# Moving five preparation pieces and thinning the feed-forward queue around steps 258 to 290 of a fused attention and feed-forward kernel

## The chip, the cores and the metric

The kernel runs on one core of a Trainium2 chip. The metric is the device time of one execution in microseconds; shown times are the median of several runs of the same kernel. TensorE does the matrix products, ScalarE the exponentials and tanh, VectorE the work on small tiles and most of what reads TensorE's results, GpSimd some element-wise work, and SyncE issues most of the transfers.

## The reference

Two parts follow each other. The first is attention in which a query only sees the keys of its own cluster; the second is a gated feed-forward layer on its output.

```python
# batch 4, heads 8, sequence 768, head size 64, 16 clusters
q_assign = argmax(normalised q . normalised centroids)      # and the same for k
scores = where(q_assign == k_assign, (q @ k.T) / sqrt(64), -1e9)
out = softmax(scores) @ v
x = out as 3072 x 512
y = (sigmoid(x @ w_gate) * (x @ w_val)) @ w_out             # 512 -> 1536 -> 512
```

## The kernel before

The work is cut into 384 **steps**, which TensorE takes in order. Batch 0 has steps 0 to 95, batch 1 has 96 to 191, batch 2 has 192 to 287 and batch 3, the last, 288 to 383. In batches 1 to 3 a pair of heads takes 24 steps: pair 0 of batch 3 begins at step 288, pair 1 at 312. A step multiplies one 128-key chunk of a head with 384 queries (tile `sc`, line 893), lets ScalarE take the exponential (`es`, line 898), and multiplies the `es` of an earlier step with V (three matmuls into `av`, line 916, two steps behind in these batches). So TensorE's order is `sc`, some feed-forward work, `av`, some preparation, and then the next step. After the last `av` of a head or head pair, VectorE and GpSimd normalise (`t` line 370, `rec` line 372, `xp` line 375), and a transposing transfer brings the result to `xTb` (line 947), the feed-forward layer's input.

**The feed-forward queue.** The feed-forward work stands in a queue of pieces, each with a cost in nanoseconds that was written by hand: `g` (four matmuls of 384 columns, line 530, then a tanh `th`, line 536), `v` (four matmuls, line 546, then a VectorE product into `hT`, line 551), and pieces of the output product (`o`, line 821, three matmuls of 256 columns each). At each step the function `ffn_run(ns)` adds `ns` to a credit and takes pieces from the queue while the credit is positive. The number is `ns` plus the batch plus the quarter of the batch: `ns23` holds for batch 2, fourth quarter, steps 264 to 287. What a step does not take stays in the queue for later steps, and what is left at the end runs after the last step; all pieces run in any case. A `g` piece of batch 2's first half is entered in the queue at step 283.5, behind the pieces that still wait there.

The output product of a half batch runs as seven products k = 0 to 6 into two long-lived accumulators, x and y; each product has four `o` pieces. Products 0, 2, 4 and 6 go to x, the others to y. Behind a product a VectorE or ScalarE operation reads the accumulator: ScalarE after k = 0, VectorE (line 768) after all others, twice after k = 4. Product 5 adds to y and so must wait until the operation behind k = 3 has read y.

**The banks.** `sc`, `g`, `v`, most small results (`lg`, line 434; `vs_ps`, line 341) share one pool of four accumulator banks (`ring`). A new tile in it waits until the reader of the tile that had the bank is done: the exponential for `sc`, the tanh for `g`, line 551 for `v`, line 449 for `lg`, line 346 for `vs_ps`.

**The preparation.** What a head pair needs before its first step is cut into named pieces, and each piece has a step offset in the table `SCHED`, relative to the first step of the pair. A name such as `b3p1lg0` is batch 3, pair 1, piece `lg` of head 0; where a batch has no entry of its own, that of batch 2 holds for batches 2 and 3. The pieces of this change are

- `lg`: twelve small matmuls (line 434) of the transposed keys and queries with the centroids. They need `T`, which a transposing transfer (line 410) brings.
- `pk`: the assignment from them, all on VectorE (lines 449, 460, 462 twice, 469), into a tile that a later piece transposes.
- `vs`, `vu`, `vt`: the sum over all V rows; `vs` is one VectorE addition (line 330), `vu` two more (lines 336 and 337), `vt` one matmul (line 341) and one VectorE operation (line 346).

Every engine takes its instructions in the order in which this program wrote them, so a piece that stands early on VectorE and waits keeps what is behind it waiting.

Of the kernel before, what the change touches and what calls it, by code (L numbers as in the profile page):

```python
# [59 lines left out]
    "b1p2vs": -11.0, "b1p2vu": -2.5, "b1p2vt": 3, "b1p2ld": -67.5, "b1p2l20": 1.5, "b1p2le0":  # L60
    2.0, "b1p2l21": 0, "b1p2le1": 2.0, "b1p3sp00": -60.5, "b1p3sp01": -54.0, "b1p3tn0": -51,
    "b1p3lg0": -38.0, "b1p3pk0": -36.5, "b1p3sp10": -55.0, "b1p3sp11": -43.0, "b1p3tn1":
    -40.0, "b1p3lg1": -29, "b1p3pk1": -27.0, "b1p3ot": -23.5, "b1p3hp0": -13.0, "b1p3hp1":
    -12.5, "b1p3vc": -7.5, "b1p3vs": -18.5, "b1p3vu": -14.5, "b1p3vt": 4, "b1p3ld": -69.5,
    "b1p3l20": 0, "b1p3le0": -4.0, "b1p3l21": 0, "b1p3le1": 1.0, "b2sp00": -57.5, "b2sp01":
    -54, "b2tn0": -49.5, "b2lg0": -39, "b2pk0": -39, "b2sp10": -50.0, "b2sp11": -44.5,
# [11 lines left out]
    "xs13": 0, "sd": 1, "b2lk": -0.5, "b1lk0": 2.0, "b1lk1": -9, "b1lk2": -0.5, "b1lk3": -1.5,  # L78
    "b2lq": 0, "b1lq0": 2.5, "b1lq1": -0.5, "b1lq2": 1.0, "b1lq3": -4.5, "b2lv": 1.0, "b1lv0":
    -1, "b1lv1": 0.5, "b1lv2": 0.5, "b1lv3": 1.5, "ns02": 490, "ns03": 490, "ns20": 500,  # L80
    "ns21": 491, "ns22": 481, "ns23": 491, "ns30": 443, "ns31": 443, "ns32": 443, "ns33": 423,
    "h6hi1E": "P", "h1ev1E": "A", "g1hi0E": "A", "h3hi1E": "P", "g1lo0E": "D", "h1lo0E": "D",
    "r3pl0E": "A", "hM3": 0, "hM7": 1, "h1hi0E": "P", "g1hi1E": "P", "h3ev0E": "A", "g0pl0E":
    "A", "g1pl0E": "A", "hM2": 1, "g1ev0E": "A", "wq": 6, "b2p1lk": 8, "b2p1lq": 8, "b2p1lv":
# [7 lines left out]
    "g0pl1E": "A", "kc": 3, "r2ev1E": "A", "g1pl1E": "A", "vso32": 1, "r0ev1E": "A", "vso31":  # L92
    1, "tx": 1, "b2p3lk": 8.5, "b2p3lq": 9, "b2p3lv": 10, "b3p3lk": 8.5, "b3p3lq": 9,
    "b3p3lv": 10,
}


# [1493 lines left out]
```

## Time and profile before

| what | us |
|---|---|
| median of 3 runs (322.22 to 323.26) | 322.86 |
| the profiled execution | 323.67 |
| its span, first to last instruction | 321.9 |
| TensorE busy | 314.6 |
| ScalarE busy | 231.1 |
| VectorE busy | 224.9 |
| GpSimd busy | 108.6 |

In the profile's rows PE is TensorE's matmul, PEld its weight load, DVE is VectorE, ACT is ScalarE, POOL is GpSimd and SP is SyncE; a q behind the name is the engine's sequencer. A row of the timeline has the start, the length, the engine, the line, the operation, the tiles it writes and reads with their shapes, and how many instructions it joins; brackets tell the idle time before it. Because matmuls overlap, a TensorE row's length reaches into the next row; what a group costs is read from one start to the next.

### The profile page before, as it was taken

Reading aid. Unit: us, or ns where it says so; the run is one execution under the profiler, and the core shown is the slowest. Engines: PE = TensorE matmul, PEld = TensorE weight load, DVE = VectorE, ACT = ScalarE, POOL = GpSimd, SP = SyncE. Lnnn points to the kernel's source line nnn. Section 1 sums busy time; section 2 is a strip of 40 time slices with the busy share of each in tenths; the row PEclk is TensorE's granted clock in tenths of the full one; section 3 lists DMA queues with packets and bytes.
Section 4 is the critical chain, followed back from the end, with each engine's and each line's share of the span. In section 5 each row is a group of like instructions: output and inputs, shape, how many; then the busy total and the mean of one; then the engine's idle time right before and its main releaser. Section 6 shows DMA issues by size and latency. Waiting matters only on the chain.

```text
span 321.9 us, 9181 instructions
## 1 busy us (share of the span) xinstructions
PE 314.6 (98%) x3510; PEld 222.4 (69%) x3510; DVE 224.9 (70%) x598; ACT 231.1 (72%) x521; POOL 108.6 (34%) x145
## 2 busy tenths in 40 slices
PE   7999999999999999999999999999999999999996
PEld 5888666766666666666777687566777688667775
DVE  5799656777787677576878587586767356456666
ACT  6688988787888888877867866778877886332320
POOL 6877464154434365433133333414211111000000
PEclk9999999999999999999999999999999999999999
DMA  7999997738876996978884751942503112200103
GB/s 214 374 256 180 244 171 118 210 75 236 238 113 187 163 238 155 223 172 136 108 219 115 217 113 33 314 110 52 111 2 90 40 26 79 77 2 1 65 2 131
DMA packets 77709, 45.16 MB, mean 140 GB/s; under 512 B 56865, under 2 KB 75105, under 8 KB 77665
## 3 DMA queue, kind: packets, MB, share of 16 engines
q1 hardware_dynamic: 73696, 39.73, 49.7%
q0 software_dynamic: 3680, 4.72, 9.0%
q8 instruction: 27, 0.44, 0.6%
q10 hardware_dynamic: 288, 0.13, 0.2%
q14 instruction: 18, 0.14, 0.2%
HBM read 28.34 MB, written 6.29 MB: 108 GB/s over the span
## 4 chain that ended last, share of the span: by engine, by line
PE 89%; DMA 3%; DVE 3%; issue 2%; POOL 1%; SPq 0%; ACT 0%; POOLq 0%; DVEq 0%
PE g L530 19%; PE v L546 19%; PE sc L893 17%; PE av L916 10%; PE o L821 8%; PE o L684 5%; PE lg L434 2%; PE o_end L594 2%; DMA T<-hl 2%; PE lg L421 1%; PE t_ps L1142 1%; PE o L594 1%; DMA xTb<-xp 1%; PE oh_ps L1202 1%; DMA qraw<-in_q_dram 1%
## 5 line engine op out<-in xcount | busy, mean ns | idle before, releaser
L898 ACT ACTIVATE es<-sc 128x384 f16<-128x384 f32 x384 | 174.3, 492 | 40.6 <-PE sc L893 31.9
L893 PE MATMUL sc<-T 128*128 128x384 f16 x384 | 117.8, 326 | 0.4 <-DVE T L1223 0.4
L916 PEld LDWEIGHTS <-es 128*128 128x128 f16 x1152 | 81.3, 98 | 35.9 <-issue 0.8
L916 PE MATMUL av<-va,es 128*128 128x65 f16 x1152 | 97.6, 194 | 0.0
L551 DVE SCALAR_TENSOR_TENSOR hT<-th,v 128x384 f16<-128x384 f32 x96 | 53.0, 553 | 55.6 <-PE av L916 36.0
L530 PE MATMUL g<-xTb,wg 128*128 128x384 f16 x384 | 78.2, 326 | 0.7 <-DMA xTb<-xp 0.5
L546 PE MATMUL v<-xTb,wv 128*128 128x384 f16 x384 | 78.1, 326 | 0.0
L536 ACT ACTIVATE th<-g 128x384 f32<-128x384 f32 x96 | 47.2, 491 | 35.0 <-PE g L530 15.9
L375 POOL TENSOR_TENSOR xp<-t,rec 128x384 f16<-128x384 f32 (+1 forms) x30 | 21.6, 720 | 101.8 <-DVE rec L372 52.3
L530 PEld LDWEIGHTS <-wg 128*128 128x128 f16 x384 | 37.2, 97 | 19.3 <-issue 0.4
L546 PEld LDWEIGHTS <-wv 128*128 128x128 f16 x384 | 37.4, 98 | 18.6
L893 PEld LDWEIGHTS <-T 128*128 128x128 f16 x384 | 37.1, 97 | 0.6 <-DVE T L1223 0.5
L1459 POOL TENSOR_TENSOR hl<-kraw,hl 128x384 f16<-128x384 f32 x22 | 20.2, 920 | 41.1 <-DVE hl L1458 20.5
L1459 POOL TENSOR_TENSOR hl<-qraw,hl 128x384 f16<-128x384 f32 x22 | 20.9, 950 | 9.8 <-DVE hl L1458 9.8
L768 DVE TENSOR_TENSOR ob<-o,ob 128x256 f32<-128x256 f32 (+1 forms) x35 | 17.8, 523 | 7.6 <-PE o L821 6.8
L370 DVE TENSOR_TENSOR t<-av,sv 128x390 f32<-128x390 f32 (+1 forms) x30 | 14.4, 479 | 9.7 <-PE av L916 7.3
L821 PEld LDWEIGHTS <-sum 128*128 128x128 f16 x168 | 16.4, 98 | 5.2 <-issue 0.8
L684 PE MATMUL o<-wo,hT 128*128 128x512 f16 x72 | 19.9, 379 | 0.0
L821 PE MATMUL o<-wo,hT 128*128 128x256 f16 x126 | 19.8, 272 | 0.0
L449 DVE TENSOR_REDUCE lgs<-lg 128x192 f32<-128x384 f32 x23 | 12.7, 551 | 2.8 <-PE lg L434 2.7
L821 PEld LDWEIGHTS <-hT 128*128 128x128 f16 x126 | 12.2, 97 | 3.4
L322 POOL CAST va<-vraw 128x768 f16<-128x768 f32 x15 | 13.0, 869 | 1.9 <-DMA vraw<-in_v_dram 1.9
(158 smaller groups left out, 340.1 us busy)
## 6 DMA issues: line engine op xcount, KB each, us to landing
vraw<-in_v_dram SPq DMA_DIRECT2D x15, 384.0 KB, 4.9
kraw<-in_k_dram SPq DMA_DIRECT2D x14, 384.0 KB, 4.3
qraw<-in_q_dram SPq DMA_DIRECT2D x12, 384.0 KB, 4.2
out_dram<-ob SPq DMA_DIRECT2D x18, 256.0 KB, 2.4
wg<-in_moe_w_gate_dram POOLq DMA_DIRECT2D x2, 768.0 KB, 9.5
wv<-in_moe_w_val_dram POOLq DMA_DIRECT2D x2, 768.0 KB, 10.3
wo<-in_moe_w_out_dram POOLq DMA_DIRECT2D x2, 768.0 KB, 9.3
T<-ohT SPq DMA_DIRECT2D x44, 24.0 KB, 1.9
```

The lines of the kernel that those rows point to most:

```text
L375: (eng or POOL).tensor_tensor(x, t[:, 0:nq, 0:64], bcast(rec[:, 0:nq], 64), ALU.mult)
L530: PE.matmul(out=g[:, 0:n], lhsT=wg[fc // WQ][:, dc, fc % WQ, :], rhs=xT[:, dc, t0 : t0 + n], start=(dc == 0), stop=(dc == NDC - 1),)
L536: ACT.activation(th[:, 0:n], g[:, 0:n], AF.Tanh)
L546: PE.matmul(out=w[:, 0:n], lhsT=wv[fc // WQ][:, dc, fc % WQ, :], rhs=xT[:, dc, t0 : t0 + n], start=(dc == 0), stop=(dc == NDC - 1),)
L551: DVE.scalar_tensor_tensor(HB[b, blk][:, fc, 0:n], st[0][:, 0:n], 1.0, w[:, 0:n], ALU.add, ALU.mult)
L684: PE.matmul(out=o, lhsT=HB[b, blk][:, fc, bass.ts(t, 128)], rhs=wo[fc // WON][:, fc % WON, :], start=(fc == 0), stop=(fc == NFC - 1),)
L768: plus = lambda dst, a, z: DVE.tensor_tensor(dst, a, z, ALU.add)
L821: PE.matmul(out=st[z][:, e], lhsT=a[:, c, :], rhs=rhs[:, c, :], start=start and c + e == 0, stop=c == HF - 1, skip_group_check=True,)
L893: PE.matmul(out=sc.rearrange("p (c t) -> p c t", t=128), lhsT=s["k"], rhs=s["q"], start=True, stop=True,)
L898: ACT.activation(es, sc, AF.Exp, scale=SCALE)
L916: PE.matmul(out=av[:, a0 + s["c0"] + i, :], lhsT=s["es"][:, bass.ts(i, 128)], rhs=VA[b, p][:, e, s["j"], :], start=(first and i == 0 and a ...
L1459: POOL.tensor_tensor(hl[:, :, 64:128], r, hl[:, :, 0:64], ALU.subtract)
```

## The change

Six entries of the table are new or changed. Nothing is computed differently; no instruction is added or left out.

```diff
-    "b1p3lg0": -38.0, "b1p3pk0": -36.5, ... "b1p3lg1": -29, "b1p3pk1": -27.0,
+    "b1p3lg0": -38.0, "b1p3pk0": -36.5, ... "b1p3lg1": -28, "b1p3pk1": -27.0,
...
-    "ns21": 491, "ns22": 481, "ns23": 491,
+    "ns21": 491, "ns22": 481, "ns23": 410,
...
+    "b3p0vs": -30, "b3p0vu": -28, "b3p0vt": -9, "b3p1lg0": -32, "b3p1pk0": -32, "END": 0,
```

In steps:

| piece | before | after |
|---|---|---|
| batch 1, pair 3: `lg1` | 139 | 140 |
| batch 3, pair 0: `vs` | 269 | 258 |
| batch 3, pair 0: `vu` | 271 | 260 |
| batch 3, pair 0: `vt` | 290 | 279 |
| batch 3, pair 1: `lg0`, `pk0` | 273 | 280 |
| credit per step, steps 264 to 287 | 491 ns | 410 ns |

The entry `END` is read by nothing. The smaller credit withholds 24 x 81 ns = 1,944 ns of hand-written cost, so that from step 265 on the queue's pieces stand later than before, by one to three steps at first; the first `g` of batch 2's first half moves from step 284 to 286, and of the last output product of batch 2 seven `o` pieces instead of three stand in step 383 or behind it.

4 rows, old and new, of the table SCHED are left out of this document.

## The prediction

> **What bounds the kernel now.** I read the page's first part, then TensorE's busy time by stretch, then the matmul rows in order, looking for places where the next start comes later than the matmul before it allows.
>
> ```profile
> PE 314.6 (98%) x3510; PEld 222.4 (69%) x3510; DVE 224.9 (70%) x598; ACT 231.1 (72%) x521; POOL 108.6 (34%) x145
> ```
> ```profile
> 184.60:204.70 20.10, 18.94 (x226) 15.06 (x225) 15.86 (x42) 13.13 (x28) 7.69 (x10) 1.00 0.48 122
> 224.00:313.00 89.00, 89.00 (x812) 62.86 (x811) 53.62 (x121) 51.30 (x112) 8.60 (x12) 1.00 0.16 45
> ```
>
> TensorE is the bound; no other engine is over 72%. In the second stretch (from step 315 on) it shows no idle time; in the first (steps 264 to 287, the ones whose queue is thinned) it misses 1.2 of 20.1 us. The order of TensorE's work changes, its amount does not, so the change can win or lose only holes, and I price it hole by hole. I first need what a step costs, from one start to the next:
>
> ```profile
> 182.74 0.81 PE L530 MATMUL g<-xTb,wg 128*128 128x384 f16 x4
> 183.38 0.26 PE L916 MATMUL av<-va,es 128*128 128x65 f16 x3
> ...
> 183.89 0.81 PE L546 MATMUL v<-xTb,wv 128*128 128x384 f16 x4
> 184.54 0.25 PE L916 MATMUL av<-va,es 128*128 128x65 f16 x3
> 184.63 0.33 PE L893 MATMUL sc<-T 128*128 128x384 f16 x1
> ```
> ```profile
> 194.68 0.49 PE L821 MATMUL o<-vheld,sum 128*128 128x256 f16 x3
> 195.78 0.49 PE L821 MATMUL o<-wo,sum 128*128 128x256 f16 x3 [0.62 <-DVE ob L768]
> 196.11 0.26 PE L916 MATMUL av<-va,es 128*128 128x65 f16 x3
> 196.20 0.32 PE L893 MATMUL sc<-T 128*128 128x384 f16 x1
> ```
> ```profile
> 200.02 0.45 PE L434 MATMUL lg<-cm,T 128*128 128x32 f16 x12
> 200.32 0.32 PE L893 MATMUL sc<-T 128*128 128x384 f16 x1
> 200.48 0.65 PE L530 MATMUL g<-xTb,wg 128*128 128x384 f16 x3
> 201.68 0.32 PE L530 MATMUL g<-xTb,wg 128*128 128x384 f16 x1 [0.54 <-DMA xTb<-xp]
> ```
>
> So g or v costs 0.65 (0.16 a matmul), an o piece 0.33 (195.78 to 196.11), av 0.09, sc 0.16 (200.32 to 200.48), lg 0.30. Two holes are already visible: in step 277 the next o could start at 194.68 + 0.33 = 195.01 and starts at 195.78, **0.77 lost**; in step 284 the fourth matmul of g could start at 200.48 + 3 x 0.16 = 200.97 and starts at 201.68, **0.71 lost**. The two others:
>
> ```profile
> 99.02 0.26 PE L916 MATMUL av<-va,es 128*128 128x65 f16 x3
> 99.41 0.36 PE L434 MATMUL lg<-cm,T 128*128 128x32 f16 x8
> ```
> ```profile
> 205.96 0.81 PE L546 MATMUL v<-xTb,wv 128*128 128x384 f16 x4
> ...
> 207.01 0.32 PE L893 MATMUL sc<-T 128*128 128x384 f16 x1
> 207.49 0.81 PE L530 MATMUL g<-xTb,wg 128*128 128x384 f16 x4
> ```
> ```profile
> 206.88 0.56 DVE hT L551
> 207.44 0.04 issue
> ```
>
> Step 139: lg could start at 99.11 and starts at 99.41, **0.30 lost**, waiting for T's transfer. Step 292: g could start at 207.17 and starts at 207.49, **0.32 lost**: its bank is that of the v two steps earlier, whose reader, line 551, ends at 207.44 (the chain of waits; 0.05 from a reader's end to the matmul). A hole under 0.16 is covered by the modelled ends of the matmuls; by the starts, the stretch from 224 us has one of 0.12 in step 322, the same kind:
>
> ```profile
> 229.46 0.49 PE L821 MATMUL o<-wo,hT 128*128 128x256 f16 x3
> 229.91 0.32 PE L530 MATMUL g<-xTb,wg 128*128 128x384 f16 x1
> ```
>
> **The change part by part.**
>
> *lg1 of batch 1, pair 3, one step later.* Step 140 holds only sc and av, so TensorE reaches lg 0.25 later, when T lacks 0.05. Gain **0.25**. pk1, which reads it, stays a step behind; it gave TensorE no hole.
>
> *lg0/pk0 and vs/vu away from the product: step 277.* The o that lost 0.77 is product 5, which waits until line 768 has read y behind product 3. VectorE's order was:
>
> ```profile
> 192.78 0.26 DVE L336 TENSOR_TENSOR va<-va 128x128 f32<-128x128 f32 x1
> 193.08 0.52 DVE L337 TENSOR_TENSOR vs<-va,va 128x128 f16<-128x128 f32 x1
> 193.52 0.55 DVE L449 TENSOR_REDUCE lgs<-lg 128x192 f32<-128x384 f32 x1
> 194.10 0.35 DVE L460 TENSOR_REDUCE mx<-lgs 128x12 f32<-128x192 f32 x1
> 194.49 0.43 DVE L462 TENSOR_TENSOR oh<-lgs,mx 128x96 f16<-128x96 f32 x2
> 194.95 0.19 DVE L469 TENSOR_SCALAR oh<-oh 128x96 f16<-128x96 f16 x1
> 195.05 1.88 DVE L768 TENSOR_TENSOR ob<-o,ob 128x512 f32<-128x512 f32 x3
> 196.85 0.35 DVE L370 TENSOR_TENSOR t<-av,sv 128x195 f32<-128x195 f32 x1
> 197.23 0.18 DVE L372 RECIPROCAL rec<-t 128x3 f32<-128x3 f32 x1
> ```
>
> From 192.78 to 195.05 VectorE does vu and pk0, 2.27 us, ahead of the 768 that TensorE waits for (its turn was over after one of the three, 0.63 each). Both leave. In the changed order product 3 ends in step 276 and product 5 begins in step 280; between them TensorE has av, all of 277 (one o, 0.58), 278 with two o (0.91), 279 with one o and vt (0.6) and sc of 280, some 2.3 us, for one 768. Gain **0.77**. If that cover went, for instance because the two sums in front of that 768 grew, up to 0.77 would come back. Late next: sc of 283 waits for vt's line 346 behind two 768 (1.26) and sc of 284 for line 449 (0.55); TensorE has about 2.4 and 3.3 us until then, so nothing.
>
> *The thinner queue: step 284.* The o pieces in front of the g are spread over two steps more, and the g itself moves to 286. Its chain begins at t in step 278: t at 196.85, landing 0.04 before 201.68, so 4.79 us, of which the transfer is the largest:
>
> ```profile
> 198.06 3.58 DMA xTb<-xp
> ```
>
> Before, t started 0.65 after sc of 278 (VectorE was at the three 768) and TensorE needed 4.8 from there to the fourth g matmul. After, with one 768 gone ahead, t can start some 0.25 after it, so landing is at about 5.0; TensorE's steps 278 to 285 sum to 0.91 + 0.64 + 0.88 + 0.58 + 0.91 + 0.88 + 0.58 + 0.58 and 286 adds 0.16 + 0.33 + 0.49 until the fourth, 6.9 in all. Gain **0.71**, with 1.9 us to spare. On SP two stores and the load of keys are issued behind this transfer, as before; the 512 KB store moves behind that load, whose keys are first read in step 304.
>
> *vt from 290 to 279: step 292.* It took a bank between v and g. Without it g of 289 and 292 wait for exponentials, as the built program has them. Gain **0.32**. At 279 there are no g and v to rob of a bank.
>
> *What vs and vu cost at their new place.* vs stands in front of a conversion that feeds a transfer needed 20 steps later; vu stands in front of line 449 of another head, whose bank sc of 264 then takes.
>
> ```profile
> L330 DVE TENSOR_TENSOR va<-vraw x12: 523/550/1175, 69.4 to 243.4; 128x384 f32<-128x384 f32 x12
> ```
> ```profile
> L337 DVE TENSOR_TENSOR vs<-va,va x12: 295/296/889, 76.0 to 247.2; 128x128 f16<-128x128 f32 x12
> ```
> ```profile
> 183.22 0.55 DVE L449 TENSOR_REDUCE lgs<-lg 128x192 f32<-128x384 f32 x1
> ```
> ```profile
> 183.59 0.49 ACT L536 ACTIVATE th<-g 128x384 f32<-128x384 f32 x1 [0.16 <-PE g L530]
> ```
>
> Line 449 moves from 183.22 to about 183.8 (0.26 + 0.30), ends at 184.35, and sc of 264 is due at 184.63: hidden; at the longest 337 (0.89) it would end 0.3 late. But the banks are dealt anew: v of step 263, due at 183.89, took the bank that line 449 had freed and now takes that of the g of 261, whose tanh ends at 184.08. It waits until 184.13. Loss **0.24** (bounds 0 and the 0.32 of step 292).
>
> *The shifted rhythm, steps 286 to 383.* All g and v stand a step or more later. In the built program one g repeats the case of step 292: g of 310 takes the bank of v of 308. From v's start to g's start that took 207.49 - 205.96 = 1.53; TensorE's own way is 0.65 + 0.09 + 0.16 + 0.09 + 0.16 = 1.15. Loss **0.38** (bounds 0, if VectorE is early, and twice that). The small hole of 322 I leave in both kernels. The seven o at the end cost what they cost elsewhere, since TensorE is the bound in both places; product 6 there comes about 1.9 us behind the two 768 that it needs (1.26).
>
> **Sum.** -0.25 - 0.77 - 0.71 - 0.32 + 0.24 + 0.38 = **-1.43 us**. The profiled execution would go from 323.67 to 322.2. The median shown is 322.86, 0.81 below it; I take the holes to be in every run and forecast 322.86 - 1.43 = **321.4 us**.
>
> **The rivals.**
>
> *The waits stay where they were.* Product 5 or the transfer is late for another reason, and the steps only wait elsewhere. For it: the 3.58 is well over what other such transfers take.
>
> ```profile
> DMA to landing us min/median/max: 2.3/2.5/4.1
> ```
>
> Against it: even 4.1 fits in the 1.9 us to spare. If one of the two large holes stays, the gain is about 0.7 and the time 322.2; if both, 322.86. Chance 0.17.
>
> *Slower: the bank wait at every turn.* The g that takes the bank of the v two steps back pays up to 0.38 each time. From step 286 to 362 a g stands two steps behind a v at thirteen places, before the change at ten. Four places beyond the one counted eat the gain; from seven on (-1.43 + 7 x 0.38 = +1.2) the kernel is slower, 324.1. For it: the wait exists at 292 and 322, and a VectorE operation in front of line 551 is enough for it. Against it: most of the ten places of before show no hole, since an o or lg in between (0.30 to 0.33) covers the wait, or the g takes the bank of an exponential. Chance 0.13. The Trainium skill's Perfetto Trace Analysis, section Identifying Performance Opportunities, says that a gap repeating on the engine that should be saturated can mean too little PSUM for the next tile; the ring keeps its four banks here, so by that rule the waits would go on and the time would be that 324.1. This case's trace agrees only in part: with the same four banks, 89.00 of 89.00 us from 224 us on show as busy.
>
> *More than forecast.* Neither new wait comes: -2.05, 320.8, or the small holes go too, 320.6. Chance 0.08.
>
> **How the numbers follow.** My forecast has 0.62. Its own range is 320.8 to 321.9: the sum with both new waits at nothing and with 0.5 more. Adding the case where large holes stay gives 322.7 above; runs of one kernel scatter by half a microsecond, which takes the low end to 320.4. A measurement tells this kernel from itself at about 0.3%, 0.97 us; the forecast is -0.44%. Faster by more than that: 0.62 + 0.08 = 0.70; within: 0.17; slower: 0.13.
>
> **What would show it.** Right: no TensorE hole over 0.1 us in steps 277 to 300; lg of 140 starting at most 0.2 behind the start of its av; the fourth g matmul of step 286 right behind the third; line 768 right behind product 3; holes of 0.2 to 0.4 at v of 263 and g of 310. Wrong: a hole at o of 280 or g of 286, or a row of holes at g between 286 and 362 with line 551 as the releaser, or transfers that land over 5.5 us after their issue.

## The result and the profile after

| | before | changed |
|---|---|---|
| median of 22 runs each, us | 322.88 (322.22 to 324.59) | 322.0 (321.42 to 323.41) |
| profiled execution, us | 323.67 | 323.41 |
| its span | 321.9 | 321.6 |
| TensorE busy | 314.6 | 314.1 |

The ratio is 0.997 with a 95% interval of 0.9957 to 0.9982, so the changed kernel is faster by about 1 us (0.003 x 322.88 = 0.97). The forecast was 321.4 us, 1.43 us faster. A later set of 12 runs of the same kernel gave 0.9962 (0.9948 to 0.9976), 1.2 us faster.

In the changed kernel all lines behind the table stand one further down than before (`g` 531, `v` 547, `hT` 552, `sc` 894, `av` 917, `lg` 435, `o` 822, `ob` 769). The page's first part of the changed kernel, then the busy time by stretch: all engines over steps 264 to 287 (the first two numbers are the stretch's length and TensorE's busy time), and TensorE alone from 224 us on:

```profile
PE 314.1 (98%) x3510; PEld 222.1 (69%) x3510; DVE 225.2 (70%) x598; ACT 230.8 (72%) x521; POOL 108.9 (34%) x145
```
```profile
185.98:202.61 16.63, 16.63 (x214) 13.85 (x213) 13.95 (x39) 11.90 (x25) 6.92 (x9) 1.00 0.49 125
```
```profile
224.00:313.00 89.00, 89.00 (x809) 1.00 0.18 45
```

Steps 264 to 287 show no idle time any more; before they missed 1.2 us. In the timeline of the changed kernel, TensorE's rows from the last piece of product 3 to the first of product 5 and around the first `g`, and VectorE's read of y behind product 3:

```profile
194.16 0.49 PE L822 MATMUL o<-kheld,sum 128*128 128x256 f16 x3
194.49 0.25 PE L917 MATMUL av<-va,es 128*128 128x65 f16 x3
194.58 0.33 PE L894 MATMUL sc<-T 128*128 128x384 f16 x1
194.74 0.49 PE L822 MATMUL o<-vheld,sum 128*128 128x256 f16 x3
...
196.71 0.33 PE L894 MATMUL sc<-T 128*128 128x384 f16 x1
196.87 0.49 PE L822 MATMUL o<-wo,sum 128*128 128x256 f16 x3
...
201.29 0.49 PE L822 MATMUL o<-wo,hT 128*128 128x256 f16 x3
201.62 0.81 PE L531 MATMUL g<-xTb,wg 128*128 128x384 f16 x4
202.26 0.26 PE L917 MATMUL av<-va,es 128*128 128x65 f16 x3
```
```profile
194.69 0.69 DVE L769 TENSOR_TENSOR ob<-o,ob 128x512 f32<-128x512 f32 x1 [0.28 <-PE o L822]
```

VectorE's read now starts right behind the product that ends at 194.7, instead of behind preparation work, product 5 starts at 196.87 without a wait (0.16 behind its `sc`), and the four matmuls of the first `g` stand in one row: its fourth no longer waits. Step 140 (start of `lg` 0.09 behind the start of its `av`) has no hole either:

```profile
99.24 0.26 PE L917 MATMUL av<-va,es 128*128 128x65 f16 x3
99.33 0.45 PE L435 MATMUL lg<-cm,T 128*128 128x32 f16 x12
```

The two new waits are where they were forecast, at `v` of step 263 and at `g` of step 310. TensorE's rows, and in a fence of its own ScalarE's tanh whose bank `v` takes, over at 185.19 (184.70 + 0.49):

```profile
184.85 0.33 PE L894 MATMUL sc<-T 128*128 128x384 f16 x1
185.25 0.81 PE L547 MATMUL v<-xTb,wv 128*128 128x384 f16 x4
...
218.55 0.33 PE L894 MATMUL sc<-T 128*128 128x384 f16 x1
219.08 0.81 PE L531 MATMUL g<-xTb,wg 128*128 128x384 f16 x4 [0.20 <-DVE hT L552]
```
```profile
184.70 0.49 ACT L537 ACTIVATE th<-g 128x384 f32<-128x384 f32 x1 [0.16 <-PE g L531]
```

By starts, less the 0.16 of `sc`, that is 0.24 and 0.37. And there is one hole that was not foreseen, in step 177, where the change moves nothing. `lg` could start at 120.52 + 0.09 = 120.61 and starts at 122.06, **1.45 lost**, for a transfer that the chain of waits (the last row) shows with 7.08 us:

```profile
120.52 0.26 PE L917 MATMUL av<-va,es 128*128 128x65 f16 x3
122.06 0.47 PE L435 MATMUL lg<-cm,T 128*128 128x32 f16 x12 [1.29 <-DMA T<-hl]
```
```profile
114.93 7.08 DMA T<-hl
```

From step 132 on the first profile had holes of 0.30 + 0.78 + 0.71 + 0.31 + 0.07 + 0.12 = 2.29 us (the fifth and sixth in steps 298 and 322), the changed one has 0.23 + 0.37 + 1.45 = 2.05. The difference, 0.24, is about what the two executions differ by (0.26). Whether step 177 belongs to the change, and which part of the change removed which hole, is what the experiments had to tell.

### The profile page after: what moved, and what is told of

Read it like the earlier page. It is cut to its first block, busy times and chain, and to the rows that moved or that the text cites. A ratio compares the mean times of both kernels' runs of the same rounds, so it can differ in the third digit from the quotient of the medians.

```text
span 321.6 us, 9181 instructions
## 1 busy us (share of the span) xinstructions
PE 314.1 (98%) x3510; PEld 222.1 (69%) x3510; DVE 225.2 (70%) x598; ACT 230.8 (72%) x521; POOL 108.9 (34%) x145
## 4 chain that ended last, share of the span: by engine, by line
PE 92%; DVE 3%; DMA 2%; ACT 1%; issue 0%; ACTq 0%; POOL 0%; DVEq 0%
PE g L531 20%; PE v L547 19%; PE sc L894 18%; PE av L917 10%; PE o L822 10%; PE o L685 3%; DMA T<-hl 2%; PE lg L435 2%; PE o_end L595 2%; PE lg L422 1%; PE o L595 1%; PE oh_ps L1203 1%; PE t_ps L1143 1%; PE wm L985 1%; PE t_ps L1026 0%
```

## The experiments

The change has seven entries that act, not six: the places of `lg1`, `vs`, `vu`, `vt`, `lg0` and `pk0`, and the credit. Holes below are worked out as in the prediction, from one start to the next, in the profile of each run, from step 132 on. Ratios are against the kernel before, run on the same chip.

**lg1 alone.**

```diff
-"b1p3lg1": -29
+"b1p3lg1": -28
```

> Only lg1 of batch 1, pair 3 is moved from step 139 to 140. Theory (holes on TensorE add up): the hole of 0.30 us at lg of 139 goes, nothing else changes, -0.3 us against the kernel before. Rival (the hole of 1.45 us at lg of step 177 in the changed kernel's profile comes from this move, because everything behind step 139 now asks its transfers 0.3 us earlier): a hole over 1 us at lg of 177 here too, and in most runs, so +0.8 to +1.2 us.

Measured: 0.9995 (0.9978 to 1.0013), no difference. In its profile (TensorE's timeline) the transfer of `T` landed later, and the hole of 139 came back in step 140: `av` starts at 99.10 and ends its 0.09 at 99.19, `lg` starts at 99.66, 0.47 lost. There is no hole in step 177. In step 284 the order is that of before and the hole is 0.41 instead of 0.71.

```profile
99.10 0.26 PE L916 MATMUL av<-va,es 128*128 128x65 f16 x3
99.66 0.47 PE L434 MATMUL lg<-cm,T 128*128 128x32 f16 x12 [0.30 <-DMA T<-hl]
```

A later place does not remove this wait for good; the landing itself moves between executions by more than the step that was won.

**All but lg1.**

```diff
 (the changed kernel)
-"b1p3lg1": -28
+"b1p3lg1": -29
```

> The changed kernel with lg1 put back to step 139. Theory: holes at 139 (0.30), 263 (0.23) and 310 (0.37), none at 177, 277, 284 and 292; -1.1 us against the kernel before, 0.3 slower than the changed kernel. Rival (the lg1 move brings the hole at 177): no hole at 177 and a kernel that is as fast as the changed one or faster than it, -1.0 to -2.0 us.

Measured: 0.9963 (0.9947 to 0.9979). Its holes are 0.39 in step 139, 0.23 in 263 and 0.37 in 310; 177, 277, 284 and 292 have none. The whole gain is there without lg1's move.

**The thinner queue alone.**

```diff
-"ns23": 491
+"ns23": 410
```

> Only the credit of steps 264 to 287 goes from 491 to 410 ns; no piece moves. Theory of the prediction (the hole of 0.77 us at step 277 goes because lg0/pk0 and vs/vu leave VectorE's queue ahead of line 768): that hole stays here, at least in part, and the kernel gains 0.71 at step 284 and little more. Rival (the thinner queue alone gives line 768 the time it needs): no hole at 277 to 280, none at 284, a bank wait of about 0.2 at v of 291 in place of the one of 292, and the 0.37 at 310; -1.2 us, nearly the whole gain of the change.

Measured: 0.9966 (0.9951 to 0.998). The rival was right: with every preparation piece at its old place, the steps from 277 to 286 have no hole. In VectorE's timeline of this kernel (first fence) `pk0` (lines 449 to 469) still stands ahead of the 768 behind product 3, as before; the second fence is TensorE's timeline there, from the last piece of product 3 on, and the third that piece in the kernel before:

```profile
193.25 0.55 DVE L449 TENSOR_REDUCE lgs<-lg 128x192 f32<-128x384 f32 x1
...
194.68 0.19 DVE L469 TENSOR_SCALAR oh<-oh 128x96 f16<-128x96 f16 x1
194.78 0.68 DVE L768 TENSOR_TENSOR ob<-o,ob 128x512 f32<-128x512 f32 x1
```
```profile
193.32 0.49 PE L821 MATMUL o<-kheld,sum 128*128 128x256 f16 x3
...
194.48 0.82 PE L821 MATMUL o<-vheld,sum 128*128 128x256 f16 x6
195.13 0.26 PE L916 MATMUL av<-va,es 128*128 128x65 f16 x3
195.23 0.32 PE L893 MATMUL sc<-T 128*128 128x384 f16 x1
195.39 0.49 PE L821 MATMUL o<-vheld,sum 128*128 128x256 f16 x3
...
195.81 0.33 PE L893 MATMUL sc<-T 128*128 128x384 f16 x1
195.97 0.49 PE L821 MATMUL o<-wo,sum 128*128 128x256 f16 x3
```
```profile
192.61 0.49 PE L821 MATMUL o<-kheld,sum 128*128 128x256 f16 x3
```

But product 5, at 195.97, comes 0.5 us after VectorE's read is over (194.78 + 0.68 = 195.46). The thinner queue moves product 3 later, past preparation that keeps its steps: `vu` is now done ahead of the product, and less of `pk0` is still to come. From the start of product 3's last piece, VectorE's read starts after 1.46 us (194.78 - 193.32) where it was 2.44 before (195.05 - 192.61). TensorE's own way from that piece to product 5 grows only from 2.40 (195.01 - 192.61) to 2.65. What is left is 0.18 in step 291, where `v` takes the bank of a tanh (sc starts at 203.53, `v` at 203.87), 0.37 in step 310 and 0.46 in step 139.

**The pieces alone, without the thinner queue and lg1.**

```diff
+"b3p0vs": -30, "b3p0vu": -28, "b3p0vt": -9, "b3p1lg0": -32, "b3p1pk0": -32,
```

> Only vs, vu, vt, lg0 and pk0 of batch 3 move; lg1 and the credit stay as before. Theory: the holes of 277 (0.77) and 292 (0.31) go, that of 284 stays at about 0.7, that of 263 (0.23) comes, none at 310; -0.85 us. Rival (the transfer at 284 is late only in some executions): a hole at 284 that differs from 0.7 by more than 0.3 in this profile.

Measured: 0.9993 (0.9978 to 1.0008), 0.2 us, where 0.85 had been expected. The hole of 277 is gone, as is that of 292, and 263 shows its 0.23. But part of the gain is lost again in 284, in TensorE's timeline and, for the transfer, the chain of waits:

```profile
199.61 0.65 PE L531 MATMUL g<-xTb,wg 128*128 128x384 f16 x3
201.18 0.32 PE L531 MATMUL g<-xTb,wg 128*128 128x384 f16 x1 [0.92 <-DMA xTb<-xp]
```
```profile
197.17 3.96 DMA xTb<-xp
```

`g` starts 0.87 us earlier than before (200.48 there), its fourth matmul only 0.50 earlier (201.68 there), because it waits for a transfer: 201.18 - 199.61 - 0.49 = 1.08 lost instead of 0.71. The transfer was issued 0.89 earlier as well (197.17 against 198.06), but took 3.96 us and not 3.58: what is gained ahead of a wait for a transfer counts only as far as the transfer lands earlier too. In three profiles with the old places of these pieces and the old credit the hole is 0.71, 0.41 and 0.11, on average 0.41. Against that, this profile gives -0.78 - 0.31 + 0.23 + 0.67 = -0.19 us, near what the runs say; as it is one profile, that the transfer is as late in most runs is argued and not shown.

**The changed kernel again.** No edit.

> The changed kernel once more, for a second profile. Theory (the hole of 1.45 us at lg of step 177 is one execution's late transfer): no hole over 0.5 us at 177, holes of 0.23 at 263 and 0.37 at 310 again, a profiled execution about 1.4 us shorter than the first; -0.9 us or more against the kernel before. Rival (the change brings it): the hole at 177 again, at 1 us or more.

Measured: 0.9962 (0.9948 to 0.9976). The profile has holes in 263 (0.23) and 310 (0.37) alone; 177 has none. TensorE's time from `sc` of step 138 to its last matmul is 219.19 us, against 220.64 in the first profile: the difference is the 1.45 of step 177.

**vt, lg1 and a queue of 420; vs, vu, lg0 and pk0 stay.** The order of the built program deals `v` of 263 and `g` of 310 other banks here, and the credit of 420 was chosen for that.

```diff
-"b1p3lg1": -29   "ns23": 491
+"b1p3lg1": -28   "ns23": 420
+"b3p0vt": -9,
```

> Of the change, lg1 at 140 and vt at 279 are kept; vs, vu, lg0 and pk0 stay where the kernel before has them, and the credit of steps 264 to 287 is 420 instead of 410 ns. Theory (the queue and vt carry the gain; vs and vu bring the bank wait at 263, and the wait at 310 comes from where exactly g and v fall): no hole at 263, 277, 284, 292 and 310, so 0.23 + 0.37 = 0.6 us faster than the changed kernel, -1.5 us or more against the kernel before. Rival (vs, vu and lg0 were needed to free VectorE for line 768): a hole of 0.3 to 0.8 at step 277 to 280 comes back and the kernel is no faster than the changed one.

Measured: 0.9957 (0.994 to 0.9974), that is 1.4 us where 1.5 or more had been expected; median 321.69 us where the changed kernel on the same chip had 322.06. The intervals of the two overlap. No hole is left in 263, 277, 284, 292 or 310. The place of the first of them in TensorE's timeline:

```profile
183.27 0.33 PE L894 MATMUL sc<-T 128*128 128x384 f16 x1
183.43 0.81 PE L547 MATMUL v<-xTb,wv 128*128 128x384 f16 x4
```

`v` starts right behind `sc` (0.16). The bank ring is as large as it was.

**The kernel before again.** No edit.

> The kernel before once more, for a second profile. The holes that a reader on VectorE ends (277, 292, 322) have the same length to 0.02 us; those that a transfer ends (139 and 284) differ from the first profile's 0.30 and 0.71 by 0.1 to 0.4.

Measured: one execution of 322.69 us. The holes that end with another engine repeat to 0.01 us: 0.79 in 277 and 0.31 in 292. Those that end with a transfer do not: 139 has none, and in TensorE's timeline the four matmuls of `g` in 284 now stand in one row, 0.76 from the first to the `av` behind them instead of 0.65, so 0.11 lost where it had been 0.71, a larger difference than the 0.1 to 0.4 expected.

```profile
194.27 0.49 PE L821 MATMUL o<-vheld,sum 128*128 128x256 f16 x3
195.38 0.49 PE L821 MATMUL o<-wo,sum 128*128 128x256 f16 x3 [0.62 <-DVE ob L768]
...
200.08 0.92 PE L530 MATMUL g<-xTb,wg 128*128 128x384 f16 x4
200.84 0.25 PE L916 MATMUL av<-va,es 128*128 128x65 f16 x3
```

**vs, vu and vt alone.**

```diff
+"b3p0vs": -30, "b3p0vu": -28, "b3p0vt": -9,
```

> Only vs, vu and vt of batch 3, pair 0 move; lg0 and pk0 stay in step 273. Theory (most of the 2.27 us ahead of line 768 is lg0/pk0 with 1.5 us, so that they alone make the hole at 277): the hole at 277 stays at 0.3 or more. Rival (any 0.8 us less on VectorE is enough): it is under 0.15. In both cases 0.23 at 263 and a hole of 0.4 to 1.1 at 284.

Measured: one execution of 321.66 us. Without vu, but with pk0, in front of the 768, step 277 loses 194.76 - 194.06 - 0.33 = 0.37, about half of the 0.77; the move of lg0 and pk0 takes the other half. TensorE's timeline:

```profile
194.06 0.49 PE L822 MATMUL o<-vheld,sum 128*128 128x256 f16 x3
194.76 0.49 PE L822 MATMUL o<-wo,sum 128*128 128x256 f16 x3 [0.20 <-DVE ob L769]
```

Step 284 has no hole in this execution, where 0.4 to 1.1 had been expected; its transfer took 2.85 us, against 3.96 with lg0 and pk0 moved as well.

**vt and a queue of 420, without lg1; and the same with lg1 again.**

```diff
 (first kernel: vt and queue only; second: as above, with lg1 at -28)
-"ns23": 491
+"ns23": 420
+"b3p0vt": -9,
```

> As the kernel with lg1, vt and a credit of 420 ns, but lg1 is back at step 139. Theory (lg1's move is worth what the hole at 139 is over many executions, 0.30, 0.39, 0.46, 0.37 and 0 in five profiles, less what remains at 140, 0, 0, 0.47 and 0 in four): 0.1 to 0.3 us slower than with lg1 at 140, so -1.1 to -1.4 us against the kernel before. Rival (the transfer's landing takes the move back in full): no difference to the kernel with lg1 at 140.

> The kernel with lg1 at 140, vt at 279 and a credit of 420 ns, beside the one without lg1. Theory: -1.4 us against the kernel before, as in its first measurement (0.9957); no hole over 0.1 us behind step 140 except the 0.17 near the end. Rival (its first measurement of seven undisturbed runs was lucky): -0.9 to -1.2 us, as the changed kernel.

Measured: 0.9951 (0.9936 to 0.9966) without lg1 and 0.9954 (0.9939 to 0.9968) with it, no difference: lg1's move does not show in the time. The first profile has one hole, 0.57 in step 139, the second one, 0.23 in step 140.

**lg1 one step later still.**

```diff
 (vt and a queue of 420)
-"b1p3lg1": -29
+"b1p3lg1": -27
```

> As before, with lg1 at step 141, where T has landed in every profile so far. Theory (the banks decide: behind lg at 141 the v of step 147 gets the bank of the v of 145, whose reader ends about 0.4 us too late): no hole at lg of 141, but one of 0.3 to 0.5 at v of 147. Rival (a bank wait read from the order of instructions does not show on the chip): none at either place.

Measured: one execution of 321.77 us. `lg` of 141 waits for nothing (`g` ahead of it starts 0.11 late). But the banks of the next steps are dealt anew and `v` of step 147 waits for line 552, 103.55 - 102.99 - 0.16 = 0.40 us, which had been read from the order of the built program. TensorE's timeline:

```profile
102.99 0.33 PE L894 MATMUL sc<-T 128*128 128x384 f16 x1
103.55 0.81 PE L547 MATMUL v<-xTb,wv 128*128 128x384 f16 x4 [0.23 <-DVE hT L552]
```

**The changed kernel a third time.** No edit.

> The changed kernel, third profile. Holes of 0.23 at 263 and 0.37 at 310 to 0.02 us. Theory (late transfer in single executions): none over 0.5 at 177; rival (the change makes T of step 177 late in every second execution): a hole of over 1 us there.

Measured: one execution of 321.88 us, with holes of 0.23 in 263 and 0.37 in 310 and none in 177.

TensorE's time from step 200 to its last matmul, which leaves out steps 139, 140 and 177 and the start-up, sums this up:

| kernel | us from step 200 to the end |
|---|---|
| before, two profiles | 183.62, 183.03 |
| lg1 alone | 183.34 |
| changed, three profiles | 182.24, 182.24, 182.25 |
| all but lg1 | 182.25 |
| queue alone | 182.19 |
| pieces alone | 183.14 |
| vs, vu and vt alone | 182.43 |
| vt and a queue of 420, four profiles with lg1 in three places | 181.64, 181.65, 181.65, 181.65 |

The two profiles of before differ by 0.59, as their holes of 284 do (0.71 - 0.11 = 0.60). The changed kernel and the last row differ by 0.60, the sum of the two waits at 263 and 310 (0.23 + 0.37).

## Why the prediction was right, and where it was not

The sign and the rough size were right: 322.0 lies in the range 320.4 to 322.7, 0.6 above the forecast and 0.1 above the forecast's own range of 320.8 to 321.9. The gain of the first set, 0.97 us, is just where the prediction put the limit of what can be told from nothing; both intervals exclude a gain of nothing. Point by point:

- **TensorE's holes decide.** Right. From step 200 on the holes account for the whole difference to 0.02 us: 183.62 - 182.24 = 1.38, and the holes of before in 277, 284, 292, 298 and 322 (0.78 + 0.71 + 0.31 + 0.07 + 0.12) less the two new ones (0.23 + 0.37) give 1.39.
- **lg1, 0.25.** Mis-sized. The hole of 139 was read from one execution. In the seven profiles with lg1 at 139 it is 0.30, 0.39, 0.46, 0.37, 0.57, 0 and 0, on average 0.30; in the six with lg1 at 140 it is 0, 0.47, 0, 0, 0.23 and 0, on average 0.12. The move is worth about 0.18 by these few profiles, less than the runs can tell from nothing.
- **Step 277, 0.77.** The sum is right, and the attribution too narrow. That VectorE's preparation held the 768 is shown: the hole goes with the pieces alone, and about half of it goes when `vs` and `vu` move and `lg0` and `pk0` stay. But the thinner queue removes it alone, with all pieces in place, because product 3 then comes later and meets less of that preparation. In the whole change each of two parts would remove this hole alone; beside the thinner queue, moving `vs` and `vu` brings only the loss of step 263.
- **Step 284, 0.71.** Right that the thinner queue removes it (it is in none of the nine profiles with a thinner queue), mis-sized by what it was: 0.71, 0.41 and 0.11 in three profiles of the same order there (before, lg1 alone, before again), on average 0.41. The prediction took 3.58 us for the transfer as fixed; in those three profiles it took 3.58, 3.28 and 2.98.
- **Step 292, 0.32.** Right. It is in every profile in which vt stands at 290 and the queue is that of before (0.31), and in none with vt at 279. With vt at 290 and the thinner queue there is one of 0.18 at `v` of 291 instead.
- **The new waits, 0.24 and 0.38.** Right: 0.23 and 0.37 in all three profiles of the changed kernel. That of 263 is in all six profiles in which `vs` and `vu` moved and in none of the other eight; that of 310 is in all five with a credit of 410 and in none with 420 or 491.
- **The small hole of 322, left in both.** Wrong: it went with the thinner queue, alone too, and so did one of 0.07 in step 298 that the prediction did not name, 0.19 together. With the pieces alone both stay.
- **The rivals.** The waits did not stay. The bank wait at every turn did not come; one `g` of thirteen paid, the one that the order of the built program names. The Trainium skill's Perfetto Trace Analysis, section Identifying Performance Opportunities, says that a gap repeating on the engine that should be saturated can mean too little PSUM for the next tile; one rival of the prediction took from the Trainium skill that the waits would go on with the same four banks. They did not: with four banks and another order, vt and a queue of 420 show no gap at 263, 292 or 310.
- **Product 5 at step 280 and the sums.** The order was as described: line 769 starts at 194.69, right behind the product.

With the measured sizes the sum is -0.18 - 0.78 - 0.41 - 0.31 - 0.19 + 0.23 + 0.37 = -1.27 us. The two sets of runs say -0.97 and -1.23, with intervals of about 0.4 us to either side. The forecast of -1.43 thus had 0.30 too much in the hole of 284, as one profile happened to show it, 0.07 too much in lg1 and 0.19 too little in the small holes. That these errors partly cancel is luck. What separates -1.27 from the first set lies within its interval.

The 1.45 us of step 177 were in one of fourteen profiles of all kernels here, one of the three of the changed one. The transfer behind it took 4.1 to 5.3 us elsewhere and 7.08 there. The prediction had named a landing over 5.5 us as a sign against it, and meant `xTb`; it came at `T`. For `T` such a landing says little: in the first profile of the kernel before, 5 of the 22 transfers of line 410 took more, 5.8 to 6.8 us. Why this one was late is open; a larger share of slow transfers in the changed kernel than in others is not shown, and could not be with three profiles.

The experiments lead to a version below both: `vt` at 279 and the queue at 420, everything else as before, 0.9951 (0.9936 to 0.9966), 321.83 us. Against the changed kernel the intervals overlap; the 0.60 us from step 200 on is what the profiles show.

## What to carry to other kernels

In this kernel a hole that ends with another engine's instruction repeated to 0.01 us, and could be forecast to 0.01 or 0.02 us from the built order; a hole that ends with a transfer is one draw, and its price must be an average over several profiles. Before crediting an edit with a hole, ask which other edit would remove it alone: here the smaller credit per step did by itself what moved pieces were credited with. Where accumulator banks go round a small ring, the list of who inherits whose bank has to be read again after every move. That holds for pieces that take no bank, too: the wait of 263 came with `vs` and `vu`.

## What the runs showed of the hardware that was not expected

- The same transposing transfer into `xTb`, behind step 278, took 2.4 us in four profiles of the full set of pieces and thin queue, 2.98 to 3.58 in three of the old order, and 3.5 to 4.2 in the five with a thin queue and lg0 at its old place. In one program alone (the kernel before) it moved between 2.98 and 3.58. What sets it was not tried.
- A long landing can belong to a place in the program. The transfer of `T` issued at about 101 us took 5.7 to 6.5 us in all fourteen profiles, and the one issued at about 80 us 3.2 to 3.3.
- Compute does not scatter like that. The wait of step 277 was 0.78, 0.79 and 0.79 us in three profiles of the same order there, and the time from step 200 on is the same to 0.01 us in three profiles of the changed kernel.
- The start-up up to step 138 took between 97.1 and 99.1 us over all profiles, a scatter larger than the whole effect; it is the same code in every kernel here.
